# Reordering the first pair's conversions, values and sums, and storing half of the last output early, in a causal convolution followed by a SwiGLU network

## The chip, the cores and the metric

The kernel runs on one core of a Trainium2 chip. The metric is the device time in microseconds, the median of several executions; lower is better. One further execution was taken by the hardware profiler, and all the profile's rows come from it. The engines are called PE (TensorE; PEld is its loading of weights), DVE (VectorE), ACT (ScalarE), POOL (GpSimd) and SP (SyncE, which here only issues DMAs).

## The reference

The input is x with 8 sequences of 4096 tokens and 192 channels, in fp32. The first stage is a causal convolution over 7 tokens with a softmax-normalized weight for each of 8 groups of 24 channels. The second stage is a network on each of the 32768 tokens: RMS normalization with a gain, two products with 192 x 1536 matrices, SiLU of one times the other, and a product with a 1536 x 192 matrix.

```python
w = weight - np.max(weight, axis=-1, keepdims=True)
w = np.exp(w); w = w / (np.sum(w, axis=-1, keepdims=True) + 1e-09)
out = np.einsum('hk,bskhg->bshg', w, x_unf)      # x_unf: the 7 last tokens of each token
rms = np.sqrt(np.mean(x * x, axis=-1, keepdims=True) + 1e-06)
xn = x / rms * rms_g
g = xn @ w_gate
silu = g * (1.0 / (1.0 + np.exp(-g)))
val = xn @ w_val
return (silu * val @ w_out).astype(np.float32)
```

The three matrices arrive as 64-bit floats and are converted to fp32 inside the kernel.

## The kernel before

The tokens are worked on in 32 pairs of two tiles of 512 tokens (T = 512, PAIRS = 32). The 1536 hidden columns are 12 blocks of 128, in four units of three.

Pair 0 is done plainly: products in `plain`, 24 groups of six matmuls (L977), the SiLU of each on ACT (L987), and the value, SiLU times the other product, on DVE (L994). A group's two PSUM banks come free with its value; there are four banks for each of the two row halves, so group n needs the banks of group n-4. Then `outer` multiplies the values with the output matrix `wo_sb` (L1017): for each token block it goes over hidden blocks f, first f = 0 to 8, later 9 to 11. Its matmuls have positions 37.5 apart; those of the second row half come 138 later. The partial results are collected by ACT (L1025) and DVE (L1029).

From pair 1 on, products use a scheme with fewer multiplications (L749, L878), on sums of token columns (`x_sum`, L667, written to `xc`) and sums of weights (`w_sums`, on POOL, L345 and L349). For these pairs the order of every engine is written out in ORDER, which is run once for each pair; a name there ends in "-" where it is work of the pair before. `Pair.do` carries out one name. At the end of a pair, C22 and C21 (L924) sum results, T22, T21, T11 and T12 turn 32 x 32 blocks into the output tile (L893), and st0 and st1 store the tile's two halves of 512 tokens, three DMAs each (L943).

While pair 0 is computed, three other things go on. First, conversion: `convert` turns 64-bit words into fp32, in steps. For the input matrices (piece "i", five steps for each of units 1 to 3): three DVE instructions (L287, L291, L294), two on ACT (L298, L299), DVE L304, DVE L314, and DVE L319, which writes `wf`. For the output matrix (pieces "o" for parts 0, 2, 4 and "O" for parts 1, 3, 5; part i holds f = 2i and 2i+1; three steps each): DVE L287, L291, L294; ACT L298, L299, L302; DVE L304 with POOL L310 and L311, which writes `wo_sb`. Parts of one piece share a buffer.

Second, the convolution and norm of the next pairs. `conv(p)` has seven taps on DVE (L418, L420), the last of which issues the load of x for the next pair. `norm(p)` has five steps: square (ACT L459), reduce (DVE L470 to L472), factor (POOL L476 to L482), spread (DVE L489), and the norm multiply (POOL L497), which writes `yn`. `y` and `yn` have one buffer each. `place(p)` writes `yn` to DRAM in eight DMAs (SP, L632), and `fetch(p)` reads it back, turned, in four (SP, L645) into `xb`; the token sums read `xb`.

Third, `out_sums`, the sums of output weights on POOL.

The order of all this is written out by hand. START is a string; each letter takes one step of a piece. Its letters: p, s, v are the product, SiLU and value of the next group of pair 0; i, o, O are the conversions; c, n and t are conv(1), norm(1) and place(1); w is w_sums; those ahead of the first f belong to the first pair's own norm. With numbers from zero, p20 is the twenty-first group and n4 the norm multiply of pair 1. LATER and the calls after it put further steps at positions on one line on which `outer` lies too; `base` is its start, and steps are issued in order of position. Each engine carries out its own instructions in the order in which they were issued and waits where one is not ready.

Of the kernel before, what the change touches and what calls it, by code (L numbers as in the profile page):

```python
# [19 lines left out]
def kernel(  # L20
# [10 lines left out]
    nc = tc.nc  # L31
# [25 lines left out]
    PAIRS = B * NB  # L57
# [9 lines left out]
    XSUM = (  # L67
        (0, 1, 4), (1, 2, 6), (2, 0, 6), (9, 3, 5), (3, 3, 8), (4, 7, 15), (5, 4, 15), (6, 5, 7),
        (7, 0, 1), (8, 1, 2), (9, 8, 15),
    )  # L70
# [166 lines left out]
    def load_out(i):  # L237
# [28 lines left out]
        out=taps[:], in0=w_sb[:], in1=stat[:].to_broadcast([P, H, K]), op=ALU.subtract  # L266
# [7 lines left out]
        out=taps[:], in0=taps[:], in1=ssum[:].to_broadcast([P, H, K]), op=ALU.mult  # L274
# [416 lines left out]
    def put(at, do):  # L691
        heapq.heappush(line, (at, next(tick), do))
# [10 lines left out]
    def copy(eng, dst, src, s=1):  # L703
        if eng == "A":
            nc.scalar.activation(out=dst, in_=src, func=AF.Copy, scale=float(s))  # L705
        elif s < 0:
            nc.vector.tensor_scalar(out=dst, in0=src, scalar1=-1.0, scalar2=None, op0=ALU.mult)
        else:
            nc.vector.tensor_copy(out=dst, in_=src)
# [13 lines left out]
    class Unit:  # L723
        def __init__(self, u):
            self.u = u
            self.ht = None
            self.bk, self.tl = {}, {}
# [92 lines left out]
    class Pair:  # L820
        def __init__(self, p):
            self.p = p
            self.units = [Unit(u) for u in range(NU)]
            self.bk, self.tl, self.o_sb = {}, {}, {}
            self.line = self.products()

        def h(self, g, f):
# [80 lines left out]
        def do(self, eng, name):  # L908
            act, *at = name.split(".")
            p, n = self.p, NM * P  # L910
            if len(at) == 2:
                self.units[int(at[1])].do(eng, act, int(at[0]))
            elif at:
                self.sum(int(act[1]), int(at[0]), eng)
            elif act == "c1":
                self.open("Y", True)
                copy(eng, self.some("Y"), self.some("X"))
            elif act in ("s7", "c2"):
                t = self.tl[act] = tiles.pop(0)
                copy(eng, t[:, 0:n], self.some("Z" if act == "s7" else "X"))  # L920
            elif act in ("C22", "C21"):
                t = self.tl["s7" if act == "C22" else "c2"][:, 0:n]
                b = "X" if act == "C22" else "Z"
                nc.vector.tensor_tensor(out=t, in0=self.some(b), in1=t, op=ALU.add)  # L924
                if b == "Z":
                    self.close(b)
            elif act in ("T22", "T21"):
                t = self.tl.pop("s7" if act == "T22" else "c2")
                self.turn(t, 1, int(act[2]) - 1)
                tiles.append(t)  # L930
            elif act in ("T11", "T12"):
                b = "Y" if act == "T11" else "X"
                self.turn(self.bank(b), 0, int(act[2]) - 1)
                self.close(b)
            elif act in ("st0", "st1"):
                g = int(act[2])
                r = p * PT + g * T
                o = self.o_sb.pop(g)[:].rearrange("p a d -> p (a d)")
                o = o.rearrange("p (b d) -> p b d", d=HP)
                for c, rows, lo, hi in ((0, LOW, 0, 8), (1, UPP, 0, 8), (2, slice(0, P), 8, 12)):  # L940
                    n = T // (hi - lo)
                    to = out[r : r + T, c * HP : (c + 1) * HP].rearrange("(b p) d -> p b d", p=n)
                    nc.sync.dma_start(out=to, in_=o[rows, lo:hi, :])  # L943
            else:
                self.ahead(eng, act)

# [16 lines left out]
    def plain(hts):  # L963


        groups = [(u, g, f) for u in range(NU) for g in (1, 0) for f in range(NF)]
        groups[0 : 2 * NF] = [(0, g, f) for f in range(NF) for g in (1, 0)]
        held = {}

        def products():  # L970
            for u, g, f in groups:
                if len(hts) <= u:
                    hts.append(big.tile([P, 2, NF, T], F32, name="ht"))
                bks = held[u, g, f] = [free[h].pop(0) for h in range(2)]
                for k in range(KP):
                    for h in range(2):
                        nc.tensor.matmul(  # L977
                            out=bank(h, bks[h])[:], lhsT=wf[u][HALF[h], k * NF + f, :],
                            rhs=xb[HALF[h], g, k, :], start=(k == 0), stop=(k == KP - 1),
                            skip_group_check=True,  # L980
                        )
                yield

        def silus():
            for i in groups:
                sg = tiles.pop(0)
                nc.scalar.activation(out=sg[:], in_=bank(0, held[i][0])[:], func=AF.Silu)  # L987
                held[i].append(sg)
                yield

        def values():
            for u, g, f in groups:
                *bks, sg = held.pop((u, g, f))
                nc.vector.tensor_tensor(  # L994
                    out=hts[u][:, g, f, :], in0=bank(1, bks[1])[:], in1=sg[:], op=ALU.mult
                )
                tiles.append(sg)
                for h in range(2):
                    free[h].append(bks[h])
                yield  # L1000

        return products(), silus(), values()
# [88 lines left out]
    def done(it):  # L1091
# [7 lines left out]


    START = (
        "XxxxxxXDdDdDTDdadTbTaTfbTakTakTakTkbkKkKkKkbkbfpoffpfsicpsvivOpsipiscvpisvpvwsicwpvs"
        "iwpvscwpsiwvpiscvipsvovpwispvswcipvwspsiwOvpsiwvipsvvpswopsvwcpsOnwonvpovnopOnOnopsOov"
    )
    LATER = (
        (-9, "t"), (54, "o"), (163, "s"),
        (233, "s"), (294, "v"), (303, "s"), (463, "w"),
        (603, "v"), (679, "O"), (742, "w"), (802, "v"),
        (816, "O"), (1017, "O"), (1302, "w"), (1582, "w"), (1861, "w"), (2141, "w"),
        (2421, "w"),  # L1110
    )
    conv_first(3, hot={4: 2, 5: 2, 6: 1})
    load(1)
# [7 lines left out]
    p, sl, v = plain(hts)  # L1121
# [25 lines left out]
    base = NU * SPAN  # L1147
# [5 lines left out]
    c = base + 200  # L1153
# [6 lines left out]
    later(norm(2), c + 1650, c + 1850, c + 2050, c + 2420, c + 2440)  # L1160
    later(place(2), c + 2450)
    xat = [c + i for i in (1660, 1730, 2060, 2130, 2200, 2270, 2340)]
    xat += [base + i for i in (2900, 2970, 3040, 3110, 3180)]
    for i, at in enumerate(xat[0 : len(XSUM)]):
        put(at, functools.partial(x_sum, i))
    later(out_sums(), *[base + 2600 + 60 * i for i in range(4 * NM)])
    emit(float("inf"))
# [3 lines left out]
    for p in range(1, PAIRS + 1):  # L1171
        now = Pair(p) if p < PAIRS else None
        for w in order:
# [5 lines left out]
            eng, name = w[0], w[1:]  # L1179
            of = now  # L1180
            if name[-1] == "-":
                name, of = name[:-1], past
# [31 lines left out]
```

## Time and profile before

| | us |
|---|---|
| median of 3 runs | 2642.21 |
| lowest, highest | 2641.62, 2646.78 |
| the profiled execution | 2638.08 |
| its span | 2636.2 |
| PE busy | 2581.8 (98%) |
| DVE busy | 2271.7 (86%) |
| POOL busy | 2091.1 (79%) |
| ACT busy | 1614.4 (61%) |
| plain products of pair 0 end | about 102.1 |
| outputs of pair 0 end | about 141.1 |
| last matmul ends | about 2628.8 |

Reading the rows: in the timeline a row has start, duration, engine, line, operation, output<-input with shapes, and a count; in square brackets stands how long the engine was idle before, and what ended the idle time. In the table of stages a row has the stage, its length, and for PE, PEld, DVE, ACT and POOL the busy time and the number of instructions, then the granted PE clock (1.00 is full), the busy share of the DMA engines and the GB/s moved. In the list of waits a row has who waited for whom, the total in us, how often, and the longest. Fp32 matmuls of 64 rows appear as several records each.

### The profile page before, as it was taken

How to read it: one execution, taken by the hardware profiler on the slowest of the kernel's cores; microseconds unless marked ns; L12 is line 12 of the kernel's file. 1: busy time of each engine (PE TensorE's matmuls, PEld its weight loads, DVE VectorE, ACT ScalarE, POOL GpSimd, SP SyncE). 2: the span in 40 equal slices, each digit the busy share in tenths (PEclk: the TensorE clock that was granted, in tenths of full speed). 3: DMA queues.
4: the chain of work that ended last, by engine and by line, in shares of the span. 5: the costliest groups of instructions: out<-in, count | busy, mean ns of one | idle time of the engine just before them, and what ended most of it. 6: DMA issues, size and time to landing. Idle time of an engine off the chain costs nothing.

```text
span 2636.2 us, 71036 instructions
## 1 busy us (share of the span) xinstructions
PE 2581.8 (98%) x29002; PEld 1878.4 (71%) x29002; DVE 2271.7 (86%) x3606; ACT 1614.4 (61%) x2964; POOL 2091.1 (79%) x1693
## 2 busy tenths in 40 slices
PE   6999999999999999999999999999999999999998
PEld 3677777776777776777776777767777777777676
DVE  8988889888888888889888888888898888988875
ACT  5375556765556765557755567655577555676554
POOL 3987788877888777888787887777887778887776
PEclk9999999999999999999999999999999999999999
DMA  6312321323312223213233222233132232132210
GB/s 142 60 35 56 63 50 39 62 38 63 63 39 49 50 51 63 55 34 62 39 63 63 42 46 54 47 63 60 33 57 47 55 63 45 44 62 38 50 38 14
DMA packets 510660, 138.01 MB, mean 52 GB/s; under 512 B 482301, under 2 KB 484861, under 8 KB 510206
## 3 DMA queue, kind: packets, MB, share of 16 engines
q1 hardware_dynamic: 509772, 133.44, 26.7%
q8 instruction: 227, 3.72, 0.6%
q14 instruction: 101, 0.82, 0.1%
q10 hardware_dynamic: 560, 0.03, 0.0%
HBM read 83.87 MB, written 49.55 MB: 51 GB/s over the span
## 4 chain that ended last, share of the span: by engine, by line
PE 89%; DVE 6%; issue 2%; POOL 1%; SPq 1%; DMA 1%; ACT 0%; DVEq 0%; POOLq 0%
PE ps L749 61%; PE ps L878 27%; DVE xc L667 1%; DVE s L470 1%; DVE o_sb L893 1%; PE ps L977 1%; POOL wf L349 1%; DVE tls L924 1%; DVE y L444 0%; SPq L1115 0%; DMA x<-in_x_dram 0%; DVE y L405 0%; POOL wo_sb L311 0%; SPq L217 0%; DMA ht<-in_moe_w_val_dram 0%
## 5 line engine op out<-in xcount | busy, mean ns | idle before, releaser
L749 PE MATMUL ps<-xc,wf 64*128 64x512 f32 x4960 | 1249.7, 592 | 17.3 <-DVE o_sb L893 16.3
L749 PEld LDWEIGHTS ps<-xc,wf 64*128 64x128 f32 x4960 | 764.2, 186 | 319.5 <-issue 117.3
L749 PE MATMUL ps<-xb,wf 64*128 64x512 f32 x2480 | 707.7, 589 | 0.0
L705 ACT ACTIVATE tls<-ps 128x512 f32<-128x512 f32 (+1 forms) x636 | 365.6, 589 | 384.7 <-PE ps L878 204.0
L793 POOL TENSOR_TENSOR ht<-ht,tile 128x512 f32<-128x512 f32 x295 | 374.8, 1277 | 277.5 <-ACT tile L786 276.1
L705 ACT ACTIVATE tile<-ps 128x512 f32<-128x512 f32 x697 | 400.0, 594 | 277.2 <-PE ps L749 166.9
L749 PEld LDWEIGHTS ps<-xb,wf 64*128 64x128 f32 x2480 | 394.7, 187 | 138.4 <-issue 38.1
L705 ACT ACTIVATE ps<-ps 128x512 f32<-128x512 f32 (+1 forms) x651 | 366.9, 578 | 53.1 <-PE ps L878 38.8
L906 POOL TENSOR_TENSOR early<-ht 128x512 f32<-128x512 f32 x279 | 378.2, 1360 | 4.9
L793 POOL TENSOR_TENSOR ht<-ht,tls 128x512 f32<-128x512 f32 x201 | 254.9, 1275 | 72.4 <-ACT tls L786 70.5
L878 PE MATMUL ps<-ht,wo_sb 128*32 128x256 f32 (+1 forms) x6944 | 308.7, 326 | 0.0
L773 DVE TENSOR_TENSOR tile<-ps,tile 128x512 f32<-128x512 f32 x373 | 255.0, 687 | 56.1 <-PE ps L749 53.5
L444 DVE SCALAR_TENSOR_TENSOR ps<-xh,tp,ps 128x512 f32<-128x512 f32 x435 | 301.7, 746 | 1.0
L878 PEld LDWEIGHTS ps<-ht,wo_sb 128*32 128x32 f32 x6944 | 215.0, 110 | 93.0 <-POOL ht L793 23.5
L878 PE MATMUL ps<-ht,x 128*32 128x256 f32 (+1 forms) x5952 | 249.2, 326 | 0.2 <-issue 0.2
L906 POOL TENSOR_TENSOR ht<-ht 128x512 f32<-128x512 f32 x186 | 247.5, 1345 | 0.0
L786 ACT ACTIVATE tile<-tile 128x512 f32<-128x512 f32 x373 | 232.9, 629 | 12.5 <-DVE tile L773 12.5
L878 PEld LDWEIGHTS ps<-ht,x 128*32 128x32 f32 x5952 | 191.7, 110 | 52.1 <-issue 0.7
L773 DVE TENSOR_TENSOR ht<-ps,tls 128x512 f32<-128x512 f32 x311 | 212.0, 682 | 0.0
L773 DVE TENSOR_TENSOR ht<-ps,tile 128x512 f32<-128x512 f32 x309 | 210.5, 681 | 0.0
L773 DVE TENSOR_TENSOR tls<-ps,tls 128x512 f32<-128x512 f32 x247 | 169.5, 686 | 28.2 <-PE ps L749 26.1
L878 PE MATMUL ps<-early,x 128*32 128x256 f32 (+1 forms) x4464 | 192.8, 326 | 0.0
(129 smaller groups left out, 3167.2 us busy)
## 6 DMA issues: line engine op xcount, KB each, us to landing
xb<-xd SPq DMA_DIRECT2D x124, 384.0 KB
xd<-yn SPq DMA_DIRECT2D x248, 96.0 KB
out_dram<-o_sb SPq DMA_DIRECT2D x186, 128.0 KB
xh<-in_x_dram SPq DMA_DIRECT2D x192, 105.0 KB
xh<-in_x_dram SPq DMA_DIRECT2D x56, 98.4 KB
ht<-in_moe_w_gate_dram SPq DMA_DIRECT2D x12, 192.0 KB
ht<-in_moe_w_val_dram SPq DMA_DIRECT2D x12, 192.0 KB
tls<-in_moe_w_out_dram SPq DMA_DIRECT2D x8, 192.0 KB
```

Source lines behind the costliest of these rows:

```text
L349: nc.gpsimd.tensor_tensor(out=t[:, d, :], in0=t[:, a, :], in1=t[:, b, :], op=ALU.add if op == "add" else ALU.subtract,)
L444: nc.vector.scalar_tensor_tensor(out=dst, in0=xk, scalar=w, in1=at, op0=ALU.mult, op1=ALU.add)
L470: nc.vector.tensor_reduce(out=ss[:], in_=sq, axis=AX.X, op=ALU.add)
L667: e.tensor_tensor(out=xc[:, d, :], in0=x_op(a), in1=x_op(b), op=ALU.add)
L705: nc.scalar.activation(out=dst, in_=src, func=AF.Copy, scale=float(s))
L749: nc.tensor.matmul(out=self.new(v, h, True) if first else self.old(v, h), lhsT=wf[self.u][HALF[h], WAT[i], :], rhs=x_op(XOP[i])[HALF[h]], ...
L773: nc.vector.tensor_tensor(out=self.hv(v) if h else t[:], in0=self.old(v, h), in1=t[:], op=plus(s))
L786: nc.scalar.activation(out=t[:], in_=src[:], func=AF.Silu)
L793: engine[eng].tensor_tensor(out=self.hv(v), in0=src, in1=t[:], op=ALU.mult)
L878: nc.tensor.matmul(out=self.bank(b)[i * Q : (i + 1) * Q, at : at + n], lhsT=left, rhs=cols, start=fresh, stop=True, skip_group_check=True, ...
L893: nc.vector.transpose(out=to[:, n, lo:hi], in_=src[:, lo * Q : hi * Q].rearrange("p (b e) -> p b e", e=Q),)
L906: engine[eng].tensor_tensor(out=dst, in0=a, in1=b, op=op)
```

## The change

In START, the last step of unit 1's weight conversion (i4) comes before the second tap (c1) and no longer after it, and the last step of unit 2's (i9) before tap c4; each with the value v2 or v8 beside it. Around the last four product groups, v18 to v21 and s20 to s22 come earlier, norm multiply n4 moves from before o6 to the very end of the string, and the last step of part 4 (o8) comes into the string. In LATER, place(1) moves from -9 to 60, as n4 now comes later; part 5 of the output matrix (O, three steps) moves from 679, 816 and 1017 to 250, 330 and 420; the last two values move from 603 and 802 to 200 and 294.

The last four of the eleven token sums move from base + 2900 to 3110 to c + 2360 to 2390, which is base + 2560 to 2590; that is before the spread (c + 2420) and norm multiply (c + 2440) of pair 2.

In the last pair, T21 and st1 are done right after C21, with T22 if it was not done; a set `past` of names keeps them from being done again at their old place. In the last pair the second of the three DMAs of st0 and st1 is issued by ACT and not by SP.

```diff
@@ class Pair
+            self.past = set()
@@ def do(self, eng, name)
             p, n = self.p, NM * P
+            if name in self.past:
+                return
+            self.past.add(name)
@@
                 if b == "Z":
                     self.close(b)
+                    if p == PAIRS - 1:
+                        for name in ("T22", "T21", "st1"):
+                            if name not in self.past:
+                                self.do(eng, name)
@@
-                    nc.sync.dma_start(out=to, in_=o[rows, lo:hi, :])
+                    q = nc.scalar if c == 1 and p == PAIRS - 1 else nc.sync
+                    q.dma_start(out=to, in_=o[rows, lo:hi, :])
@@
     START = (
-        "XxxxxxXDdDdDTDdadTbTaTfbTakTakTakTkbkKkKkKkbkbfpoffpfsicpsvivOpsipiscvpisvpvwsicwpvs"
-        "iwpvscwpsiwvpiscvipsvovpwispvswcipvwspsiwOvpsiwvipsvvpswopsvwcpsOnwonvpovnopOnOnopsOov"
+        "XxxxxxXDdDdDTDdadTbTaTfbTakTakTakTkbkKkKkKkbkbfpoffpfsicpsvivOpsipisvicpsvpvwsicwpvs"
+        "iwpvscwpsiwvpisvicpsvovpwispvswcipvwspsiwOvpsiwvipsvvpswopsvwcpsvOnwovnpsovnopsOvnOopsOoon"
     )
     LATER = (
-        (-9, "t"), (54, "o"), (163, "s"),
-        (233, "s"), (294, "v"), (303, "s"), (463, "w"),
-        (603, "v"), (679, "O"), (742, "w"), (802, "v"),
-        (816, "O"), (1017, "O"), (1302, "w"), (1582, "w"), (1861, "w"), (2141, "w"),
-        (2421, "w"),
+        (60, "t"), (163, "s"), (200, "v"), (250, "O"), (294, "v"), (330, "O"), (420, "O"),
+        (463, "w"), (742, "w"), (1302, "w"), (1582, "w"), (1861, "w"), (2141, "w"), (2421, "w"),
     )
@@
-    xat += [base + i for i in (2900, 2970, 3040, 3110, 3180)]
-    for i, at in enumerate(xat[0 : len(XSUM)]):
+    xat += [c + i for i in (2360, 2370, 2380, 2390)]
+    for i, at in enumerate(xat):
         put(at, functools.partial(x_sum, i))
```

## The prediction

> **What bounds the kernel now.** I read the page first (which engine is full), then stages of 2 us around the end of the plain products, the waits there, the timeline of each engine, and the last 15 us. On the page:
>
> ```profile
> span 2636.2 us, 71036 instructions
> PE 2581.8 (98%) x29002; PEld 1878.4 (71%) x29002; DVE 2271.7 (86%) x3606; ACT 1614.4 (61%) x2964; POOL 2091.1 (79%) x1693
> ```
>
> TensorE sets the time. From pair 1 to the last it hardly waits, and the diff leaves ORDER alone; so only the first 145 us and the tail after the last matmul can move. The stages of the first pair (PE busy, PEld, DVE, ACT, POOL, then granted clock, DMA share, GB/s):
>
> ```profile
> 102.00:104.00 2.00, 1.27 (x9) 0.97 (x6) 1.97 (x2) 0.00 (x0) 2.00 (x2) 1.00 0.00 0
> 104.00:106.00 2.00, 0.00 (x0) 0.00 (x0) 2.00 (x4) 1.13 (x3) 0.90 (x2) 1.00 0.40 87
> 106.00:108.00 2.00, 1.78 (x16) 1.78 (x17) 2.00 (x4) 1.70 (x4) 2.00 (x2) 0.75 0.71 153
> 110.00:112.00 2.00, 2.00 (x14) 2.00 (x16) 1.97 (x3) 0.00 (x0) 2.00 (x2) 0.50 0.04 9
> 114.00:116.00 2.00, 2.00 (x28) 2.00 (x26) 2.00 (x3) 0.00 (x0) 2.00 (x2) 1.00 1.06 227
> ```
>
> PE stops, and then runs at half clock from 107.0 to 113.6 (14 matmul records in 2 us instead of 28). Why it stops is in the timeline:
>
> ```profile
> 95.91 1.28 DVE L994 TENSOR_TENSOR ht<-ps,tile 128x512 f32<-128x512 f32 x2
> ...
> 100.70 2.84 POOL L497 TENSOR_TENSOR yn<-y,s 128x1536 f32<-128x1536 f32 x1
> 100.77 2.99 DVE L287 TENSOR_SCALAR xc<-tls 128x384 uint32<-128x384 uint32 x1 [1.82 <-POOL wo_sb L311]
> ...
> 105.49 0.68 DVE L994 TENSOR_TENSOR ht<-ps,tile 128x512 f32<-128x512 f32 x1
> ...
> 106.22 2.86 PE L1017 MATMUL ps<-wo_sb,ht 64*128 64x192 f32 x18 [2.95 <-DVE ht L994]
> ...
> 108.10 1.61 POOL L311 TENSOR_TENSOR wo_sb<-xc 128x384 f32<-128x384 f32 x1
> ...
> 109.77 2.61 PE L1017 MATMUL ps<-wo_sb,ht 64*128 64x192 f32 x14 [0.69 <-POOL wo_sb L311]
> ```
>
> Value v20 (105.49) frees the bank that the first output matmul takes; it stands behind conversion o6, whose first instruction (100.77) sat under the norm multiply n4 (L497). Then PE waits for wo_sb rows of f=8 (o8, ready 109.71). The end of this stage:
>
> ```profile
> PE ps L749 <- DVE xc L667: 0.8, 1, 0.8
> ```
>
> That is the last token sum, done at 143.05: VectorE stood 3.33 us before L489 (136.95), and one sum took 3.27 us (139.86) under the second norm multiply (POOL 139.34, 3.30). The tail:
>
> ```profile
> 2628.84 0.65 DVE L893 STREAM_TRANSPOSE o_sb<-ps 128x256 f32<-128x256 f32 x2 [1.30 <-PE ps L878]
> 2629.32 4.01 SPq L943 DMA_DIRECT2D out_dram<-o_sb  x6
> 2629.41 0.60 DVE L893 STREAM_TRANSPOSE o_sb<-tls 128x256 f32<-128x256 f32 x2
> ```
>
> All six stores of both halves are issued after the last matmul; data flows 2630.5 to 2634.95, 0.79 MB at 150 to 236 GB/s.
>
> **The skill.** The Trainium skill, TensorE: Matmul & The Clock Gate, Part 1, says that after an idle window of about 3.4 us the clock is halved, that a busy window restores it, and that the windows run free. The trace agrees on the size (two drops begin at 28.5 and 107.0, 23 windows of 3.413 apart) but is stricter: the window before 107.0 held 0.8 us of work and still counted as idle. SBUF — State Buffer, SBUF: two separate sides, says VectorE in a two-port mode or with two SBUF inputs and GpSimd lock each other out for a whole instruction; L287 at 2.99 instead of 0.36 (97.57) during L497 agrees. DMA: Bandwidth & Descriptors, Issuing engines are not separate DMA queues, says that SP and ACT feed the same DMA engines, so that a second issuer saves issue time alone; the kernel before shows 0.6 us for an issue on SP, and no large store from ACT.
>
> **The change part by part.**
>
> *i4 before c1, i9 before c4 (VectorE).* The weights of units 1 and 2 come 2 us earlier. PE waited 0.89 and 1.12 us for L319 there. I follow p6 to p23 with 2.57 us a group and each bank released by its value: PE ends the plain products at about 101.0 instead of 102.06. Value on the end: nothing, as conversions bound what follows; cover gone, 1.0 us.
>
> *v18 to v21 and s20 to s22 up, n4 down.* VectorE after c6 (ends 89.80): v18 0.6, o2's end 0.7, o3 1.7, v19 0.6 (93.4), n1 2.2 (95.6), v20 0.6 (96.2; s20 is done at 93.8 or 95), o5 0.5, O3 1.05, v21 0.65 (98.4), n3 98.95. The 2.95 us wait for v20 is gone. o6 needs its buffer from POOL's L311, as before at 100.75; POOL's next instruction L310 (1.2) gets the port first, so o6 takes 101.9 to 102.95, O5's end 103.45. POOL: L311 of O5 to 104.5, then o8's two, 1.2 each as in rows 103.44 and 105.71: 106.7 (bounds 105.6 and 108). So f=8 is ready at 106.7 instead of 109.71. What is late next: PE starts the outputs at 101.0, waits about 1.4 us for f=6 (O5) and 1.5 for f=8, and goes on at 106.7 against 109.77. From there it took 31.33 us to 141.10, of which 3.83 ran at half clock, worth 1.9: 29.4 at full clock, so the outputs end at 136.1.
>
> *n4 behind all of it.* POOL does n4 106.7 to 109.6 (2.84; 6 us later). Queued behind it on SP are place(1)'s 8 DMAs and fetch(1)'s 4. Before, from the end of n4 (103.57) to landed data (120.1) took 16.5 us: now 126.2. y has one buffer, so conv(2) also waits for n4: VectorE idles from about 106.5 to 109.6, then 13.4 us of taps (as before, 107.67 to 124.54 less the 3.4 of other instructions): 123.0. The first token sum waits for the fetch until 126.2 (before: 125.01). O8 now comes earlier on VectorE but behind n4 on POOL, by 114.3 at worst (2.3 + 2.4 as at 116.31 and 118.66), needed at n=37, about 116.3: hidden.
>
> *All eleven sums before n3 of the next norm.* From 126.2: two sums 1.7, eviction 0.5, reduce 2.2, five sums 4.3, four 3.2 (0.8 to 0.9 each, no norm multiply over them): 138.1. The third product of pair 1 starts then, against 143.28. The first pair gains **5.1 us**; if the port waits go well (f=8 at 105.6) 6.2, badly (108) 3.8. The second norm multiply still follows n3, now at 138, before its old 139.34. Pair 1's other engines are not late: VectorE then waited 1.78 for PE, and POOL 5.09.
>
> *Tail.* T21 (0.60) goes into VectorE's idle 3.27 us before T12; its three stores go out from 2624.2, under the last 4.5 us of matmuls. After T11 three stores remain, two on SP and one on ACT, which has nothing left. Issue 4.01 becomes 2 x 0.60; data 4.45 us becomes 2.2 for half, the rate being the limit. Gain **2.2 us**, between 1.5 (rate lower with less in flight) and 3.0 (issue was the limit). ACT's issue cost isn't shown; at SP's 0.6 or double it the rate still sets the end.
>
> Sum: 5.1 + 2.2 = 7.3 us. Against the profiled span 2636.2: 2628.9; against the profiled time 2638.08: 2630.8; that execution is 4.1 under the median 2642.21, which is what is predicted: **2634.9**.
>
> **Rivals.**
> - Half clock again. PE's idle comes as 1.4 + 1.5 us with 0.66 of work between, about as empty as the window that fell before; it depends on where the free window lies. Then 2.95 us of the outputs are lost: they end at 139.05, the third product at 140.2; gain 3.1 + 2.2, 2636.9.
> - The conversions meet no port waits: f=8 by 105.6 and data by 125: gain 6.3 + 2.7, 2633.2.
> - The gain of the first pair is taken back by the sums: the fetch lands at 131 (place or n4 5 us later than worked out); only the tail stays: 2640.0.
> - Slower: n4 as last of START. If it starts at T instead of 106.7, fetch, sums and pair 1 move with it; at T = 114.0 all is spent, at 119.3 it is 0.2% slower, 2648 at 120. POOL conversions at 2.3 to 2.4 each, as two were, and VectorE's L287 at 2.99 would give 113 to 114. Against it: those two met four taps, which now stand behind n4.
>
> **How the numbers follow.** Chances: forecast 0.50, half clock 0.22, no port waits 0.10, fetch late 0.11, slower 0.07. A measurement of this kernel can hardly tell 0.2% (5.3 us) from nothing. Faster by that: nine tenths of the forecast's, half of half clock's, all of the third's: 0.66; same 0.27; slower 0.07. Range: 2631.0 (6.2 + 3.0, and 2 of scatter, as 2641.62 to 2646.78 shows) to 2640.0 (fetch late).
>
> **What would show it.** Right: no PE wait for L994 after the plain products; two waits for L311 of 1 to 2 us; clock 1.00 to 114; L497 starting at 106 to 107, place at once after; the first sum waiting for DMA; the third product at 138; three stores in the last 5 us, ACT issuing one. Wrong: L497 after 110, half clock, PE waiting for sums by over 2 us, or the tail over 6 us after the last matmul.

## The result, and the profile after

The changed kernel takes 2639.74 us, the median of 20 runs (2634.26 to 2643.67); the kernel before, run beside it on the same chip, 2642.80 (20 runs, 2638.90 to 2646.78). The ratio is 0.9985, with a 95% interval of 0.9978 to 0.9992: by the ratio 4.0 us faster, between 2.1 and 5.8 (the medians are 3.1 apart). The forecast was 7.3 us less, which lies outside that interval, and it gave 0.66 to more than 0.2% faster, where 0.15% came. The direction and the way were right; the sum was too large. The time alone would not show even that: 2639.74 is near the slow end of the range, and near the 2640.0 of the rival in which only the tail's gain stays. That the first pair gains too, the traces and the run first_only below have to show.

The page of the changed kernel (span, then busy time, share and instructions of each engine):

```profile
span 2634.5 us, 71038 instructions
PE 2580.7 (98%) x29002; PEld 1858.2 (71%) x29002; DVE 2266.0 (86%) x3606; ACT 1615.0 (61%) x2964; POOL 2089.6 (79%) x1693
```

The profiled execution took 2636.28 us, only 1.8 less than the profiled one of before (2638.08); the experiments have to say why. The stages around the end of the plain products (columns as before: PE, PEld, DVE, ACT, POOL, clock, DMA share, GB/s):

```profile
102.00:104.00 2.00, 1.66 (x19) 1.36 (x15) 1.97 (x4) 0.54 (x2) 0.81 (x1) 1.00 0.00 0
104.00:106.00 2.00, 0.45 (x6) 0.45 (x8) 1.69 (x4) 1.32 (x3) 1.70 (x2) 1.00 0.00 0
106.00:108.00 2.00, 0.89 (x10) 0.59 (x10) 1.97 (x3) 0.21 (x1) 1.92 (x3) 1.00 0.00 0
110.00:112.00 2.00, 2.00 (x28) 2.00 (x27) 2.00 (x4) 0.98 (x2) 0.69 (x2) 1.00 0.08 19
```

PE still idles about 3 us, but in two pieces, and the clock stays at 1.00: from the start of the first output matmul of pair 0 to that of the last it is 35.56 us (101.55 to 137.11), where it was 39.45 (101.81 to 141.26). The timeline of all engines for the same stretch:

```profile
101.80 1.00 POOL L310 TENSOR_TENSOR xc<-xc,tls 128x384 f32<-128x384 f32 x1
101.87 1.15 DVE L287 TENSOR_SCALAR xc<-tls 128x384 uint32<-128x384 uint32 x1 [1.56 <-POOL wo_sb L311]
...
105.56 0.92 PE L1026 MATMUL ps<-wo_sb,ht 64*128 64x192 f32 x8 [1.90 <-POOL wo_sb L311]
106.54 0.99 POOL L311 TENSOR_TENSOR wo_sb<-xc 128x384 f32<-128x384 f32 x1
107.50 3.00 POOL L497 TENSOR_TENSOR yn<-y,s 128x1536 f32<-128x1536 f32 x1
107.59 4.66 PE L1026 MATMUL ps<-wo_sb,ht 64*128 64x192 f32 x54 [1.11 <-POOL wo_sb L311]
107.67 3.03 DVE L294 TENSOR_SCALAR xc<-tls 128x384 uint32<-128x384 uint32 x1
```

PE no longer waits for a value (L1003 here); both of its waits are for POOL's L311, 1.90 us for f = 6 and 1.11 for f = 8. POOL's L310 and VectorE's o6 became ready together; POOL was first, and the first instruction of o6 took 1.15 us where it took 2.99 under the norm multiply. That multiply (L497) now stands behind the last conversion and sits on another VectorE instruction (L294, 3.03), which nobody is waiting for. The end of the stage:

```profile
128.84 0.83 DVE L667 TENSOR_TENSOR xc<-xb 128x512 f32<-128x512 f32 x1 [2.98 <-DMA xb<-xd]
...
139.83 1.53 PE L749 MATMUL ps<-xc,wf 64*128 64x512 f32 x3 [1.28 <-DVE xc L667]
139.93 0.24 DVE L489 STREAM_TRANSPOSE s<-s 128x64 f32<-128x64 f32 x1 [0.25 <-POOL s L482]
140.10 0.98 DVE L1038 TENSOR_TENSOR o_sb<-ps,o_sb 128x384 f32<-128x384 f32 x2
```

The sums wait for the fetch until 128.84 and end at 139.69; the third product of pair 1, the one that needs the last of them, starts at 139.83, against 143.28. Behind the sums, and behind the spread L489, stand the last two collections of pair 0's outputs (L1038, which adds PSUM results to the output). The weight loads show who waits for those:

```profile
140.67 0.18 PEld L749 LDWEIGHTS ps<-xc,wf 64*128 64x128 f32 x1 [0.58 <-DVE o_sb L1038]
141.21 0.19 PEld L749 LDWEIGHTS ps<-xb,wf 64*128 64x128 f32 x1 [0.17 <-DVE o_sb L1038]
...
144.30 0.29 PEld L749 LDWEIGHTS ps<-xc,wf 64*128 64x128 f32 x2 [0.59 <-DVE tile L709]
```

PE wants the PSUM banks that L1038 is still to read; at 144 us it waits for L709, VectorE's work on pair 1's own products. Last, the tail, from the timeline of all engines:

```profile
2623.76 0.64 DVE L894 STREAM_TRANSPOSE o_sb<-tls 128x256 f32<-128x256 f32 x2
2624.23 6.46 SPq L952 DMA_DIRECT2D out_dram<-o_sb  x4
2624.23 5.83 ACTq L952 DMA_DIRECT2D out_dram<-o_sb  x2
...
2628.95 0.65 DVE L894 STREAM_TRANSPOSE o_sb<-ps 128x256 f32<-128x256 f32 x2 [1.30 <-PE ps L879]
```

The first transposes (L894) and three of the six stores are issued 4.4 us before the last matmul starts (the two rows of stores count early and late ones together); from that start to the span's end it is 5.88 us, before 7.72.

### The profile page after: what moved, and what is told of

Read it like the earlier page. It is cut to its first block, busy times and chain, and to the rows that moved or that the text cites. A ratio compares the mean times of both kernels' runs of the same rounds, so it can differ in the third digit from the quotient of the medians.

```text
span 2634.5 us, 71038 instructions
## 1 busy us (share of the span) xinstructions
PE 2580.7 (98%) x29002; PEld 1858.2 (71%) x29002; DVE 2266.0 (86%) x3606; ACT 1615.0 (61%) x2964; POOL 2089.6 (79%) x1693
## 4 chain that ended last, share of the span: by engine, by line
PE 90%; DVE 6%; issue 2%; DMA 1%; ACT 0%; POOL 0%; DVEq 0%; SPq 0%; POOLq 0%; ACTq 0%
PE ps L749 61%; PE ps L879 27%; PE ps L986 2%; DVE xc L667 1%; DVE s L470 1%; DVE o_sb L894 1%; DVE tls L928 1%; PE ps L1026 1%; DVE y L444 0%; DMA x<-in_x_dram 0%; DMA xb<-xd 0%; DVE y L405 0%; DVE y L393 0%; DVE s L471 0%; PE ps L593 0%
## 5 line engine op out<-in xcount | busy, mean ns | idle before, releaser
L749 PE MATMUL ps<-xc,wf 64*128 64x512 f32 x4960 | 1254.7, 592 | 16.6 <-DVE o_sb L894 15.2
```

The lines of the kernel that those rows point to most:

```text
L749: nc.tensor.matmul(out=self.new(v, h, True) if first else self.old(v, h), lhsT=wf[self.u][HALF[h], WAT[i], :], rhs=x_op(XOP[i])[HALF[h]], ...
```

## The experiments

Positions in profiles of different kernels shift with the start: the first plain product starts at 36.94 in before and at 38.23 in after, though nothing ahead of it is changed (x arrives 0.8 us later, and an early half clock lasts two windows of the clock and not one; the last section says what a window is). So I count from that first product ("from the first product" below), and I follow single matmuls by their place in the sequence: the one that starts at 200 us in before, and the one at 300.

The column of the half clock tells for how long the clock was halved in the outputs of pair 0.

| kernel | third product of pair 1, from the first product | matmul of 200 us, from the first product | last matmul's start to span's end | half clock in the outputs |
|---|---|---|---|---|
| before | 106.34 | 163.07 | 7.72 | 6.8 us |
| tail_only | 106.24 | 162.97 | 5.88 | 6.8 |
| sums_only | 105.02 | 162.05 | 7.73 | 6.8 |
| start_only | 107.62 | 166.38 | 7.72 | none (6.8 us from 143.9) |
| first_only | 102.16 | 160.06 | 7.76 | 6.8 |
| after | 101.60 | 159.14 | 5.88 | none |
| n4_early | 104.55 | 161.58 | 5.89 | 6.8 |
| evict_first | 101.22 | 159.65 | 5.91 | 3.4 |
| place_two | 102.31 | 160.41 | 5.88 | 6.8 |
| both | 101.74 | 158.96 | 5.87 | none |
| spread_last | 101.70 | 158.78 | 5.90 | none |
| tail_sp | 101.94 | 159.34 | 5.70 | 3.4 |

My theory (A): the lead of the first pair and that of the tail are real and stay to the end; the profiled execution of before merely ran its later pairs faster than usual. The rival (B): a lead of the first pair melts in the pairs that follow, since something slower than PE catches up there.

### tail_only and first_only: each half of the change alone

tail_only keeps the edits in `Pair` and has START, LATER and the sums of before; first_only is the other way round. Both are shown against the changed kernel; what stands in brackets sums up lines left out.

```diff
 tail_only:
+    (START and LATER as before)
-    xat += [c + i for i in (2360, 2370, 2380, 2390)]
+    xat += [base + i for i in (2900, 2970, 3040, 3110, 3180)]
 first_only:
-                    q = nc.scalar if c == 1 and p == PAIRS - 1 else nc.sync
+                    nc.sync.dma_start(out=to, in_=o[rows, lo:hi, :])
-                    (if p == PAIRS - 1: T22, T21, st1 after C21; and `past`)
```

> Only the last pair's edit (T21 and the stores of the second half after C21, one store of three on ACT); the first pair as before. Theory A (the two gains add up: first pair about 3.5 us by the end of pair 1, tail 1.8, measured from last matmul to end of span, 7.43 against 5.63 us): 1.8 us faster than before, 2641.0 for a before of 2642.8, and the last matmul to the end in 5.6 us. Theory B (the lead of the first pair melts in pairs 2 to 5, where the profile of the changed kernel went from 2.6 us ahead at 300 us to 0.4 ahead at 560 us, so that the tail is the whole gain): the same 1.8 here, but as fast as the changed kernel. The two are told apart together with the next run.

> Only the first pair's edits (conversions, taps, values, norm multiply, sums); the tail as before. Theory A: 2.5 to 4 us faster than before, the lead at 300 us (2 to 3.5 us) still there at 2500 us. Theory B: within 1 us of before; the lead at 300 us gone at 600 us.

tail_only: 2640.34 against 2642.51, ratio 0.9992 (0.9983 to 1.0), some 2.1 us less, just at the edge of the interval; in the trace 1.84 us at the tail and nothing before it. first_only: 2639.62, ratio 0.9987 (0.998 to 0.9993), 3.4 us less by the ratio, between 1.8 and 5.3: the first pair does gain. The halves sum to 5.5, inside the interval of the whole.

tail_only also decides about the profiles. It has no lead at 300 us (the same matmul starts at 300.01 in both), so there is nothing to melt, and yet its last matmul starts at 2631.22, where that of before starts at 2628.50. From the 300 us matmul to the last one before took 2328.5 us, and the eleven other profiles 2330.1 to 2334.7. The execution of before that was profiled is the shortest of all in the loop. One place where it differs, PE's timeline of before, then of after and of tail_only, at the same eight matmuls:

```profile
382.63 1.99 PE L749 MATMUL ps<-xc,wf 64*128 64x512 f32 x8
```

```profile
381.27 1.99 PE L749 MATMUL ps<-xc,wf 64*128 64x512 f32 x8 [0.39 <-DVE o_sb L894]
```

```profile
383.81 1.99 PE L749 MATMUL ps<-xc,wf 64*128 64x512 f32 x8 [0.92 <-DVE o_sb L894]
```

After waits here for transposes of the output (L894) that in before's profile came in time, and so does tail_only, whose first pair is that of before. So as the explanation of 1.8 us between the profiles, B falls. The test that was set, first_only's lead against the profile of before, misleads for the same reason: counted from the first product the lead is 3.0 us at 300, 0.9 at 600 and gone (-0.4) at the last matmul. Against tail_only's profile 2.2 of 2.9 us are there at the last matmul, and of after's lead all (3.8 at both places). These are single executions, so that a smaller melting stays open.

### start_only and sums_only: the two edits of the first half

start_only changes START and LATER alone; sums_only moves the four token sums alone. Both are shown against the kernel before.

```diff
 start_only:
+    (START and LATER as in the change)
 sums_only:
-    xat += [base + i for i in (2900, 2970, 3040, 3110, 3180)]
-    for i, at in enumerate(xat[0 : len(XSUM)]):
+    xat += [c + i for i in (2360, 2370, 2380, 2390)]
+    for i, at in enumerate(xat):
```

> The conversions, taps, values and the norm multiply in the changed order, the four last token sums at their old place behind the next norm's spread; tail as before. My theory says that the later norm multiply makes these four sums a must to move: the spread waits for POOL until about 139 us, the sums come after it and under the second norm multiply, and the last ends at 145 to 148 us; third product of pair 1 at 145 to 148 instead of 143.3, so 2 to 4 us slower than before. Rival: the sums' place is of no matter, as PE has other products first; then 2 to 4 us faster than before, as with the sums moved.

> Only the four last token sums moved ahead of the spread; all else as before. The sums then end at about 137.5 us, but the outputs of pair 0 end at 141.1 as before: the third product comes at 142.3 instead of 143.3, a gain of 0.8 us, of which the two evictions that now wait behind the sums take nothing, since PE is later than they are: 0 to 1 us faster. Rival: the sums alone are the gain of the first pair: 3 us faster.

start_only is slower than before: 2647.18, ratio 1.0019 (1.0012 to 1.0026), or 3.2 to 6.9 us, more than the 2 to 4 expected. Its VectorE and then PE, from their timelines:

```profile
140.33 0.25 DVE L489 STREAM_TRANSPOSE s<-s 128x64 f32<-128x64 f32 x1 [2.27 <-POOL s L482]
...
143.22 3.27 DVE L667 TENSOR_TENSOR xc<-xc 128x512 f32<-128x512 f32 x1
```

```profile
146.64 2.08 PE L749 MATMUL ps<-xc,wf 64*128 64x512 f32 x4 [7.30 <-DVE xc L667]
```

The fetch is later now, the last sums still stand behind the spread, which waits 2.27 us for POOL, and one of them lies under the norm multiply (3.27 us for 0.83). PE is 7.30 us without work, and pays again: half clock from 143.9 for two windows, which I had not counted and which takes the loss from 1.3 us at the third product to 3.3 at 200 us. sums_only: 2640.56, ratio 0.9993 (0.9985 to 1.0002); its products are 1.0 to 1.3 us earlier (0.8 expected), though the timing cannot tell that from nothing. So the new START alone costs 5 us, the sums alone bring about 1 by the trace, and together they bring 3.4: with n4 last, the fetch sets the sums, and only sums that nothing stands in front of turn the earlier outputs into earlier products.

### n4_early: the norm multiply before the last conversion again

```diff
-        "...OvnOopsOoon"
+        "...OvnOnopsOoo"
-        (60, "t"),
+        (-9, "t"),
```

> The changed kernel with the norm multiply n4 and place(1) at their old place, before the last conversions. My theory: POOL then does n4 at 101 to 104 us, the conversions of parts 3 and 4 follow 3 us later, PE waits for f=6 and f=8 until 109 to 110 us and falls to half clock; the outputs end at 141 to 143 us, the sums, whose data now land 6 us earlier, no longer bind: third product at 142 to 144 us, as before the change, and 3 us slower than the changed kernel (2642). Rival: it is the values' order alone that gives the first pair's gain: third product at 139 to 140, as fast as the changed kernel.

The timeline of all its engines:

```profile
102.53 2.85 POOL L497 TENSOR_TENSOR yn<-y,s 128x1536 f32<-128x1536 f32 x1
102.62 2.97 DVE L287 TENSOR_SCALAR xc<-tls 128x384 uint32<-128x384 uint32 x1 [1.56 <-POOL wo_sb L311]
...
108.81 1.19 PE L1026 MATMUL ps<-wo_sb,ht 64*128 64x192 f32 x8 [4.37 <-POOL wo_sb L311]
```

The pair of instructions of before is back, 2.85 and 2.97 us side by side, and PE's 4.37 us for f = 6 bring the half clock. The third product is 3.0 us later than in after, and of the first pair's 4.7 us 1.8 are kept (sums_only alone has 1.3); that is the expected mechanism, and the values' order alone does not bring the gain. The time, 2640.62 (ratio 0.9989, 0.9981 to 0.9997), is less bad than the 2642 I expected, since the tail's part and that of the sums stay; it can't be told from the changed kernel's.

### place_two: is it the issue of place that makes the fetch late?

In after the eight DMAs of place take SP 6.32 us (before 5.25), and from the end of n4 to the first sum it is 18.3 us (before 16.5 to landed data). Here ACT issues every second one, and place comes later in LATER.

```diff
-            nc.sync.dma_start(out=to[h], in_=y[h::H])
+            q = nc.scalar if p == 1 and h % 2 else nc.sync
+            q.dma_start(out=to[h], in_=y[h::H])
-        (60, "t"),
+        (425, "t"),
```

> The changed kernel with the eight DMAs of place(1) split between SP and ACT, and place(1) moved behind the last conversion so that ACT does not stall on it. My theory: in the changed kernel the sums wait 3.0 us for the fetch because the norm multiply is 6.5 us later than before, and 6.3 us of the 18.3 from its end to landed data are the issue of eight DMAs by one engine. Halved, the data land 2 to 3 us earlier, the first sum starts at 126 to 127 instead of 128.8, and PE's outputs (end at 137.4) bind next: third product at 137.5 to 138.5 instead of 139.8, 1.3 to 2 us faster than the changed kernel. Rival: the transfer, not the issue, sets the landing (0.6 to 0.76 of the DMA engines were busy during place): less than 0.5 us earlier, no difference.

SP's part of its timeline:

```profile
112.00 4.37 SPq L633 DMA_DIRECT2D xd<-yn  x4
...
118.62 3.20 SPq L646 DMA_DIRECT2D xb<-xd  x4
```

From the end of n4 (111.97) to the first sum (129.06) it is 17.1 us. With all on SP it is 17.2 in evict_first, 17.5 in first_only, 18.3 in after and 18.9 in tail_sp; with the split again, 18.0 in both (next run). So the split brings at most 0.1 us over the best kernel without it, and the time is 2640.01 (0.9988, 0.9982 to 0.9995): the rival was right, the transfer sets this and not its issue. It is what the Trainium skill states under DMA: Bandwidth & Descriptors, Issuing engines are not separate DMA queues.

The 18.3 and the 16.5 do not end at the same thing. By the DMA packets in the traces, the last data of the fetch come 16.6 us after the end of n4 in before, 16.2 to 18.0 in the eight kernels with n4 last, 17.2 in after. The first sum starts another 0.9 to 1.2 us after the last packet (1.1 in after). In before VectorE was busy elsewhere until 125.01, so that its profile did not show this step. The rest of the difference lies ahead of the fetch, which SP issues 8.3 us after the end of n4 in after and 7.3 in before, first_only and evict_first, so it is not the changed order as such.

### evict_first and both: the collections before the last sums

```diff
-    later(norm(2), c + 1650, c + 1850, c + 2050, c + 2420, c + 2440)
-    later(place(2), c + 2450)
+    later(norm(2), c + 1650, c + 1850, c + 2050, base + 2895, base + 2896)
+    later(place(2), base + 2897)
-    xat += [c + i for i in (2360, 2370, 2380, 2390)]
+    xat += [base + i for i in (2890, 2891, 2892, 2893)]
-    later(out_sums(), *[base + 2600 + 60 * i for i in range(4 * NM)])
+    later(out_sums(), base + 2600, *[base + 2900 + 40 * i for i in range(4 * NM - 1)])
```

> The changed kernel with the four last token sums, the spread and the norm multiply of pair 2 put just behind the third eviction of the outputs instead of before it; the same order otherwise. My theory: in the changed kernel pair 1 loses 0.8 us after its third product because PE waits for a bank that the third eviction, now behind the sums, frees (rows with the wait on DVE o_sb, 0.6 us and 0.2 us, at 140.7 and 141.2 us). Here the eviction runs at about 136 us and that wait is gone: the lead kept at 200 us is 0.6 to 0.9 us more, against the third product's time, than in the changed kernel. In the median 0.7 us faster than the changed kernel, which the timing alone can hardly tell. Rival: the loss has another cause (ACT, loads of weights): the lead at 200 us does not change.

The edit missed its aim. Its VectorE timeline and its list of waits (who waits for whom: total, times, longest):

```profile
135.61 0.54 DVE L1038 TENSOR_TENSOR o_sb<-ps,o_sb 128x384 f32<-128x384 f32 x1
...
141.23 0.52 DVE L1038 TENSOR_TENSOR o_sb<-ps,o_sb 128x384 f32<-128x384 f32 x1
```

```profile
DVE s L489 <- POOL s L482: 2.0, 1, 2.0
...
PEld ps L749 <- DVE o_sb L1038: 1.5, 1, 1.5
```

The third collection moved ahead of the last sums (135.61). The fourth did not: the spread now stands before it and waits 2.0 us for POOL's factor, so the bank is held until 141.75, and at 200 us the kernel is no earlier than after (159.65 to 159.14, with one window of half clock). Time 2639.37 (0.9988, 0.998 to 0.9996).

both is evict_first and place_two in one.

> evict_first and place_two together. If both theories hold: third product at 137.5 to 138.5, no wait for the eviction, 2 to 2.8 us faster than the changed kernel, about 2637.3, 0.2% under before. If the landing is set by the transfer: 0.7 us at most.

2638.94 (0.9983, 0.9976 to 0.999). At 200 us it is 0.2 us ahead of after, so hardly more than nothing. Against evict_first it is 0.7 us ahead, but there its clock stayed full and that of evict_first did not, so that this can't be put down to an edit.

### spread_last: the spread and norm multiply behind the collections

If the spread is what holds the collections, it must go behind them:

```diff
-    later(norm(2), c + 1650, c + 1850, c + 2050, c + 2420, c + 2440)
-    later(place(2), c + 2450)
+    later(norm(2), c + 1650, c + 1850, c + 2050, base + 3790, base + 3791)
+    later(place(2), base + 3792)
```

> The changed kernel with the spread and the norm multiply of pair 2 (and place(2)) put behind the last eviction of the outputs, and so behind the sums of output weights on POOL; the sums as in the changed kernel. The last run showed that not the third but the fourth eviction, behind the spread that waits for POOL's factor, holds the bank (141.2 us, PE waits 0.6). My theory now: with the spread behind both evictions these run directly after the sums, PE waits for neither, and the time from the first plain matmul to the matmul that stood at 200 us in the kernel before falls from 159.1 us (changed kernel, full clock) or 160.1 (half clock) to 158.3 or 159.3. Rival: pair 1 is slower for another reason, or the late norm multiply costs more at pair 1's first values: 159.1 or more, and slower by 300 us.

Its waits around the third product:

```profile
PE ps L749 <- DVE xc L667: 1.3, 1, 1.3
PEld ps L749 <- DVE o_sb L1038: 0.2, 1, 0.2
```

The longer of the two weight-load waits for L1038 is gone, and the matmul of 200 us comes 0.36 us earlier than in after, not the 0.8 expected: this kernel too loses 0.24 us at the loads that wait for L709 (144 us) and 0.11 at about 195. The second norm multiply starts at 148.69 (after: 141.92), and nothing suffers from that up to 300 us. Time: 2638.23 against 2643.58, ratio 0.9979 (0.9973 to 0.9986), 3.7 to 7.1 us less than before. It has the lowest ratio of all and is clearly below before; against the changed kernel the intervals overlap, so that a gain over that one is not shown.

### tail_sp: does ACT as second issuer matter?

```diff
-                    q = nc.scalar if c == 1 and p == PAIRS - 1 else nc.sync
+                    q = nc.sync
```

> The changed kernel with all stores of the last pair on SP, the early ones still early. In ten profiles the start of the last matmul to the end of the span is 5.9 us with the changed tail and 7.7 with the old one. If the transfer sets the end, as the prediction said, it is 5.9 to 6.2 here too; if the issue does (three times 0.6 us on one engine instead of twice), 6.5.

With all stores on SP it is 5.70 us from the last matmul's start to the end, with ACT 5.87 to 5.91 in seven profiles. The second issuer saves nothing: the transfer of the second half (2630.7 to 2633.3 in after) sets the end. There is one execution of this kernel, at 2639.74 us, which says nothing of the median.

## Why the prediction was right, and where it was not

**The 2.95 us wait for v20, and n4 down.** As worked out. The first product comes 1.3 us later than in before, so 1.3 is to be taken off to compare with the forecast. The prediction had o6's first instruction at 101.9 to 102.95 (101.87 to 103.02, or 100.6 to 101.7), f = 8 ready at 106.7 (107.50, or 106.2; its own sum, 104.5 and twice 1.2, is 106.9) and waits of 1.4 and 1.5 us (1.90 and 1.11). So the waits came as forecast, and the times within 1.3 us. n4 started when the last conversion was done. n4_early shows that its move is worth 3.0 us at the third product.

**i4 and i9.** The plain products took 63.7 us from first to last instead of 64.5; 1.0 was forecast. All nine profiles with the new START have 63.7 to 63.9 and the three with the old one 64.5, but no run here separates i4 and i9 from the other letters.

**"n4 behind all of it": data at 126.2.** The first sum started at 128.84, or 127.5 without the late start: the term "end of n4 to landed data, 16.5" measured 17.2, and a term of 1.1 from the last data to the start of the waiting sum was left out (place_two). The next term made up for more than half of it, by luck: the sums took 10.85 us and not 11.9. Third product at 101.60 from the first product against 101.16 forecast: a gain of 4.7 us for 5.1.

**"Pair 1's other engines are not late".** This is the step that failed: it put at nothing what the moved sums push back. I followed the sums to PE and stopped there. Behind the sums, on the same engine, stand the spread and the last two collections of pair 0, and PE needs their banks for the next products. By 200 us 3.9 of the 4.7 us are left. Followed matmul by matmul, 0.44 of the 0.8 us go between the third and the fourth product, at the waits for L1038; in spread_last, where the longer of these waits is gone, that loss is too. The other 0.38 us go at 144 us, where weight loads wait for pair 1's L709, and at about 195; spread_last has them as well, and what causes them stays open. With the step fell "the second norm multiply before its old 139.34": it starts at 141.92, 140.6 without the late start.

**Tail 2.2 us.** Right in its mechanism (the rate limits, the second issuer does not); the term measured 1.84, alike in seven profiles with the tail's edits.

**The half clock, 0.22.** Too low as far as eight profiles tell, and its price was put in the wrong place. Of eight profiles with the new START as it stands, four have it in the outputs, by the phase of the windows (last section). There the outputs take 37.2 us (one window) or 38.1 to 38.2 (two) instead of 35.6. But the third product is only 0.3 to 0.7 us later (first_only, place_two, tail_sp; evict_first has its sums elsewhere), because the sums end just then anyway: the forecast charged all of 2.95 us (measured: 2.6) where the sums cover most. Its reading of before is 0.2 us short: the half clock there lasted to 113.8 and not 113.6.

**The sum against the profile.** Of the 7.3 us, 0.4 fall away in the first pair, 0.8 behind it and 0.4 at the tail; 3.9 and 1.84, or 5.8 us, are left at full clock; with half clock first_only is 0.9 us behind after at 200 us, and tail_sp 0.2. Timed, it is 4.0 (2.1 to 5.8), so that up to 1.8 us have no cause shown. The two profiles differ by 1.8 alone since before's loop from 300 us on was 2.7 us shorter than after's and its start 1.3 us earlier. The forecast's last step, the offset of 4.1 us between profile and median carried over to the changed kernel, did not hold: after's profile is only 3.5 under its median.

**What stays open.** In after, both, evict_first and place_two the timed gain is some 1 to 2 us under what the trace shows at 200 us and at the tail together, and start_only loses some 1.7 us more than its trace; in tail_only, first_only, sums_only, n4_early and spread_last the two agree within 1 us. The intervals are 3 to 4 us wide. The loop took 2328.5 to 2331.2 us in the three profiles with the old START and 2331.2 to 2334.7 in the nine with the new one, which leans towards B in little, but these are twelve executions. So a small melting in the loop, or a start that comes late more often (all nine profiles with the new START have the first product 1.1 to 2.7 us later than before, but sums_only, with the old one, has too), is neither shown nor excluded.

## What to carry to other kernels

When a step is moved to the front of an engine's queue, follow all that it pushes back to its own users, the collections that free PSUM banks too; here 0.4 of 4.7 us went that way. When a wait moves from an engine to a DMA, count up to the start of the waiting instruction and not to the last data; here that was 0.9 to 1.2 us. Two edits may be worth less than nothing apart (START alone: 5 us slower) because the later one removes the wait that the first creates. And where a change is worth 0.2%, compare traces at the same instruction counted from the same event, not by their spans: two executions of the same loop differ here by as much as the change is worth.

## What was not expected of the hardware

The Trainium skill, TensorE: Matmul & The Clock Gate, Part 1, has the clock halved after an idle window of about 3.4 us and restored by a busy one, the windows running free. The runs agree on the windows: the drop (to half clock) in the outputs begins a whole number of windows of 3.413 us after the one at the start (23 in first_only, 28.6 and 107.2, in evict_first, 29.4 and 107.9, and in tail_sp, 29.7 and 108.2; 24 in n4_early, 27.4 and 109.3). So the phase at the start tells which window PE's idle of 1.9 and 1.1 us falls into, read to about 0.1 us. "Idle" turns out to mean about half idle: with 1.8 to 1.95 us of 3.4 idle in one window the clock fell in first_only, place_two, evict_first and tail_sp, but not in start_only (1.91), nor in windows at the start of before (1.87), tail_sp (1.84) and tail_only (1.83); with 1.7 us or less it did not fall (after 1.7, spread_last 1.6, both 1.6). "Busy" means nearly all: where the first window at half clock still had 0.7 to 1.0 us of PE waiting (before 0.69, first_only 0.75, place_two 1.00) the half clock lasted two windows, and where it had none (evict_first, tail_sp) one. So did the half clock at the start of before and evict_first, whose window had 0.2 and 0.5 us of waiting: the limit lies between 0.5 and 0.7 us here. One window cost the outputs 1.7 us, two cost 2.6.

The loop over pairs 1 to 31 is identical in all these kernels but for the stores of the last pair. From the 300 us matmul, about two pairs in, to the last it took between 2328.5 and 2334.7 us: 0.27%, more than the whole change.
